# An RWKV-5 and MLP kernel on one core: k transposed by TensorE in all chunks, weights loaded one place later

## The chip, the core and the metric

The kernel runs on one core of a Trainium2 chip. The core has TensorE (PE, matrix products and transposes, results in PSUM banks), VectorE (DVE), ScalarE (ACT), GpSimd (POOL) and SyncE (SP, which here only issues DMAs), and 16 DMA engines that all its queues share. The engines run side by side, each through its own instructions in program order, and wait for one another by semaphores. The metric is the device time of the whole kernel in microseconds (us), as the median of several runs.

## The reference, cut to what matters

```python
# r, k, v: (4, 8, 768, 48); w, u: (8, 48)
for t in range(S):
    kt, vt, rt = k[:, :, t], v[:, :, t], r[:, :, t]
    cur = einsum('bhd,bhe->bhde', u[None] * kt, vt)
    y[:, :, t] = einsum('bhd,bhde->bhe', rt, state + cur)
    state = w[None, :, :, None] * state + einsum('bhd,bhe->bhde', kt, vt)
x = y.transpose(0, 2, 1, 3).reshape(4, 768, 384)
xn = (x - mean(x)) / sqrt(var(x) + 1e-06) * g_ln
out = x + maximum(xn @ w_ch1, 0.0) @ w_ch2      # 384 -> 1536 -> 384
```

A linear attention with a decaying state, then a LayerNorm and a two-layer MLP with a residual. Inputs and output are float32; the kernel multiplies in bfloat16.

## The kernel before, in words

The 4 x 768 tokens are cut into 24 chunks (also called tiles) of 128 tokens, six for each batch entry, with all 8 heads in a chunk. For chunk i:

- SyncE (in a few cases ACT) issues the loads of k and v, 192 KB each, and for every second chunk one of r (384 KB, two chunks): `load`, L182 and L188.
- k is scaled by powers of the decay into one of four buffers `sc` (`scale_k`, L359), r likewise (`scale_r`, L362). GpSimd or VectorE does it. v is cast to bfloat16 (`cast_v`, L368).
- k and r are transposed. For r, TensorE does 8 transposes for two chunks into the PSUM bank "tr" (`transposes_r`, L392), and ACT or VectorE copies them out as `rT` (L398). For k there are two ways. In chunks 0 to KP - 1 TensorE does 4 transposes into "tr" (chunk 0: bank "y"; `transposes_k`, L377) and ACT or VectorE copies them to `kT` (`evacuate_k`, L381). In chunks KP and up one DMA on SyncE's queue transposes the buffer straight into `kT` (`transpose_k_by_dma`, L385). KP is 14.
- TensorE multiplies kT and rT to scores ("at", L412). VectorE or GpSimd forms the product q (L405) for the bonus term, TensorE sums it (L433), ACT copies it out (L444), and GpSimd multiplies it with v to `Vb` (L448). VectorE masks the scores to `A` (two halves, L423). TensorE updates the state (L455, L464), VectorE decays it to `Z` (L475). TensorE forms the output y of the chunk (L487, L499), VectorE mixes it with Vb to x (L512).
- ACT centers x to `xn` (L525) and takes the squares (L532), GpSimd the reciprocal deviation `rs` (L538, L541). xn is transposed to `xT`: in tiles below LNP = 8 by TensorE through bank "tr" (L563, copied out at L575), in the others by a DMA on SyncE's queue (`ln_by_dma`, L571).

The MLP works on groups of tiles: six groups of one tile, then nine of two. Up projection in pieces of one PSUM bank "hp" (`up`, L588), ReLU on ACT (L599), down projection in three pieces per tile (`down`, L614), then VectorE combines with rs and x (L624) and SyncE or ACT issues the store (L635). One such up or down piece takes 0.65 us of TensorE.

w_ch1 and w_ch2 come in three loads of 768 KB each (`load_w1` L210, `load_w2` L214) on SyncE's queue. Their pieces are scaled or cast to bfloat16 by whichever of ACT, VectorE and GpSimd is chosen (L343 or L341 for w1, L353 for w2).

Nothing in this order is left to the hardware. The class `Planner` (L17) holds a list of tasks, each with an engine (some with alternatives), an estimated cost, what it needs, which buffers it takes and gives back, and a priority. `order` repeatedly picks the task that can start first by these estimates, fixes its engine, and so writes out one order for each engine. The tasks `TK`, `kT`, `sck` and `lc` of the change are added in the loop at L683. Bank "tr" has one buffer: transposes of r, of k and of LayerNorm rows follow one another in it, each after the copies of the one before. Where the planner sees a gap on TensorE before the first down projection, it puts filler matmuls on the identity there (`keep_warm`, L261).

The loads go in a fixed order, `seq` (L657). N1 and N2 say at which place in the list of r, k and v loads the three loads of w1 and the three of w2 are put in:

```python
N1, N2 = 8, 13
seq[N2:N2] = [("w2l", n) for n in range(NW)]
seq[N1:N1] = [("w1l", n) for n in range(NW)]
```

The list begins r0, k0, v0, k1, v1, r2, k2, v2, k3, v3, r4, k4, v4, k5, v5 (a load of r is named by the first of its two chunks). With 8, w1 stands between v2 and k3; with 13, w2 stands between v4 and k5.

Of the kernel before, what the change touches and what calls it, by code (L numbers as in the profile page):

```python
# [16 lines left out]
class Planner:  # L17
# [12 lines left out]
    def add(self, name, eng, cost, fn, needs=(), takes=(), gives=(), pri=0, load=0.0, kind=None,  # L30
            alt=None, lands=1.9):

        t = dict(name=name, eng=eng, cost=cost, fn=fn, needs=list(needs), takes=list(takes),
                 gives=list(gives), pri=pri, load=load, kind=kind, alt=alt, lands=lands, end=None,
                 first=(eng, cost))
        self.tasks.append(t)
        assert name not in self.by_name, name
        self.by_name[name] = t  # L40
# [79 lines left out]
def kernel(  # L120
# [249 lines left out]
    def k_bank(i):  # L370
        return "y" if i < 1 else "tr"

    def transposes_k(i):
        sc = k_bufs[i % NSC].rearrange("p (q e) d -> p q (e d)", e=2)
        tk_t[i] = ps.tile([P, 2 * HP, P], BF16, name=k_bank(i))
        for q in range(HP):
            nc.tensor.transpose(out=tk_t[i][:, q, :], in_=sc[:, q, :], identity=ident[:])  # L377
# [173 lines left out]
    PM = FK // NM  # L551
    NH = 8
    LNP = 8
    KP = 14
    ot_t = {}

    def ln_transposes(i):
# [97 lines left out]


    seq = [(a, i) for e in range(NT // 2) for a, i in (("r", 2 * e), ("k", 2 * e), ("v", 2 * e), ("k", 2 * e + 1), ("v", 2 * e + 1))]  # L657
    N1, N2 = 8, 13
    seq[N2:N2] = [("w2l", n) for n in range(NW)]
    seq[N1:N1] = [("w1l", n) for n in range(NW)]  # L660
    FS = FK // NW
# [21 lines left out]
    for i in range(NT):  # L683
# [8 lines left out]
        if not half:  # L692
# [7 lines left out]
            alt=[("DVE", 0.74)])  # L700
        if i < KP:
            add(f"TK{i}", "PE", 0.24, lambda i=i: transposes_k(i), [f"sck{i}"], [(k_bank(i), ("k", i), 1)], [("sck", i)], pri=p0)
# [97 lines left out]
```

## Time and profile before

| | us |
|---|---|
| median of 5 runs | 162.99 (162.59 to 164.77) |
| profiled execution, time | 162.66 |
| profiled execution, span | 160.9 |

The profile is one execution. Its page gives the busy time of each engine, a table of 40 slices, the DMA queues, the chain of work that ended last, and groups of instructions: line, engine, operation, output <- inputs, shapes, count, then busy time, mean duration in ns of one, idle time of the engine before them and what ended most of it. Some groups that the change touches, as the page has them:

```profile
L359 POOL TENSOR_TENSOR sc<-k,Fk 128x384 bf16<-128x384 f32 x21 | 22.0, 1046 | 5.0 <-PE s L464 3.2
L405 DVE TENSOR_TENSOR q<-rT,kT 128x512 bf16<-128x512 bf16 x21 | 13.8, 660 | 3.6 <-DMA kT<-sc 2.9
L398 ACT COPY rT<-tr 128x512 bf16<-128x512 bf16 x18 | 13.0, 736 | 3.5 <-PE tr L392 1.9
...
wst<-in_moe_w_ch_dram SPq DMA_DIRECT2D x6, 768.0 KB, 7.6
...
xT<-xn SPq DMA_TRANSPOSE x16, 3.4
```

The last two are DMA issues: output <- input, the queue (SPq is SyncE's), count, size and the median time from issue to landing. Matmuls overlap one another, so the mean duration of one is longer than the distance between two. Four transposes of k (L377) pass in 0.22 us, with 0.220 us as the duration of each.

### The profile page before, as it was taken

The page shows a single profiled execution, that of the slowest core. Times are in us where ns is not written, and L with a number is a line of the kernel's source. Part 1 is how long each engine was busy: PE and PEld are TensorE (multiplying, and loading weights), DVE is VectorE, ACT ScalarE, POOL GpSimd, SP SyncE. Part 2 cuts the span into 40 slices and gives each one's busy share as a digit, 9 for nine tenths or more (in the row PEclk, how much of TensorE's full clock was granted, in tenths as well). Part 3 has the DMA queues.
Part 4 walks back from the last instruction along what each step waited for, and adds up shares of the span by engine and source line. Part 5 has one row for each costly group of instructions (what it writes and reads, how often), then busy time and mean ns, then how long its engine had stood idle before and what let it go on. Part 6 is the DMA issues. An engine that isn't in the chain of part 4 may idle for free.

```text
span 160.9 us, 4644 instructions
## 1 busy us (share of the span) xinstructions
PE 147.2 (91%) x1825; PEld 115.7 (72%) x1825; DVE 104.2 (65%) x221; ACT 102.4 (64%) x231; POOL 92.6 (58%) x139
## 2 busy tenths in 40 slices
PE   5999999699699999999996999569999999999990
PEld 5888798487488787777784787457787777776660
DVE  5779886777898679887995998857851011111322
ACT  3577896979569859678766768476666755533200
POOL 7379796587979569996988786987331000000000
PEclk9999999999999999999999999999999999999999
DMA  4999899998998999999899797764203221111122
GB/s 108 229 218 389 240 213 357 304 203 183 253 267 187 221 230 213 187 228 160 192 209 168 156 200 175 160 133 107 78 2 98 77 73 49 49 49 53 49 98 98
DMA packets 80859, 26.78 MB, mean 166 GB/s; under 512 B 75072, under 2 KB 79686, under 8 KB 80838
## 3 DMA queue, kind: packets, MB, share of 16 engines
q1 hardware_dynamic: 77046, 25.11, 68.8%
q10 hardware_dynamic: 3696, 1.38, 4.2%
q8 instruction: 14, 0.23, 0.6%
q14 instruction: 7, 0.06, 0.2%
q0 software_dynamic: 96, 0.01, 0.0%
HBM read 18.88 MB, written 4.72 MB: 147 GB/s over the span
## 4 chain that ended last, share of the span: by engine, by line
PE 53%; DMA 17%; SPq 12%; POOL 7%; DVE 4%; issue 3%; ACT 1%; DVEq 0%; POOLq 0%; ACTq 0%
PE o L614 21%; PE hp L588 19%; SPq L188 7%; DMA kT<-sc 6%; DMA wst<-in_moe_w_ch_dram 6%; DMA v<-in_v_dram 3%; SPq L182 3%; POOL sc L359 3%; PE hp L614 2%; PE at L412 2%; DMA k<-in_k_dram 2%; POOL Vb L448 2%; SPq L210 1%; PE y L499 1%; PE tr L392 1%
## 5 line engine op out<-in xcount | busy, mean ns | idle before, releaser
L588 PE MATMUL hp<-xT,w_sb 128*128 128x256 bf16 (+1 forms) x540 | 58.1, 251 | 0.2
L599 ACT ACTIVATE hT<-hp 128x512 bf16<-128x512 f32 x72 | 42.8, 598 | 19.8 <-PE hp L588 19.1
L614 PE MATMUL o<-w_sb,hT 128*128 128x384 bf16 x264 | 52.4, 326 | 1.0 <-POOL w_sb L353 1.0
L588 PEld LDWEIGHTS <-w_sb 128*128 128x128 bf16 x540 | 43.6, 98 | 8.0 <-POOL w_sb L343 0.6
L614 PEld LDWEIGHTS <-hT 128*128 128x128 bf16 x288 | 26.7, 98 | 13.5 <-issue 0.8
L624 DVE SCALAR_TENSOR_TENSOR ot<-o,rs,x 128x384 f32<-128x384 f32 x22 | 13.5, 613 | 33.7 <-PE o L614 33.5
L423 DVE TENSOR_TENSOR A<-at,mask 128x512 bf16<-128x512 f32 x48 | 31.0, 681 | 1.8 <-PE at L412 1.8
L359 POOL TENSOR_TENSOR sc<-k,Fk 128x384 bf16<-128x384 f32 x21 | 22.0, 1046 | 5.0 <-PE s L464 3.2
L448 POOL TENSOR_TENSOR Vb<-v,cc 128x384 f32<-128x384 f32 x24 | 21.1, 878 | 5.7 <-ACT cc L444 5.6
L525 ACT ACTIVATE xn<-x,sum 128x384 bf16<-128x384 f32 x24 | 14.8, 616 | 4.2 <-DVE x L512 4.2
L512 DVE SCALAR_TENSOR_TENSOR x<-y,Vb 128x384 f32<-128x384 f32 x24 | 13.2, 551 | 5.4 <-POOL Vb L448 3.3
L405 DVE TENSOR_TENSOR q<-rT,kT 128x512 bf16<-128x512 bf16 x21 | 13.8, 660 | 3.6 <-DMA kT<-sc 2.9
L398 ACT COPY rT<-tr 128x512 bf16<-128x512 bf16 x18 | 13.0, 736 | 3.5 <-PE tr L392 1.9
L532 ACT ACTIVATE sq<-x,sum 128x384 bf16<-128x384 f32 x24 | 14.6, 609 | 0.5 <-DVE x L512 0.5
L362 POOL TENSOR_TENSOR sc<-r,Fr 128x384 bf16<-128x384 f32 x12 | 12.6, 1050 | 3.7 <-ACT Fr L303 2.9
L541 POOL TENSOR_TENSOR rs<-rs,expo 128x1 f32<-128x1 f32 x24 | 13.5, 564 | 2.0
L261 PE MATMUL o<-ident 128*128 128x128 bf16 x154 | 12.7, 238 | 1.6 <-DVE ident L236 1.6
L412 PE MATMUL at<-rT,kT 48*128 48x128 bf16 x192 | 9.5, 219 | 2.8 <-DMA kT<-sc 2.8
L261 PEld LDWEIGHTS <-ident 128*128 128x128 bf16 x154 | 10.5, 108 | 1.9 <-DVE ident L236 1.6
L475 DVE TENSOR_TENSOR Z<-s,WLZ 128x384 bf16<-128x384 f32 x20 | 11.0, 548 | 0.3 <-ACT cc L444 0.2
L362 DVE TENSOR_TENSOR sc<-r,Fr 128x384 bf16<-128x384 f32 x12 | 9.7, 805 | 0.4 <-ACT Fr L303 0.3
L538 POOL TENSOR_SCALAR rs<-sqs 128x1 f32<-128x1 f32 x24 | 5.3, 221 | 7.6 <-ACT sq L532 6.1
(81 smaller groups left out, 173.4 us busy)
## 6 DMA issues: line engine op xcount, KB each, us to landing
r<-in_r_dram SPq DMA_DIRECT2D x12, 384.0 KB, 4.6
k<-in_k_dram SPq DMA_DIRECT2D x24, 192.0 KB, 4.1
wst<-in_moe_w_ch_dram SPq DMA_DIRECT2D x6, 768.0 KB, 7.6
v<-in_v_dram SPq DMA_DIRECT2D x21, 192.0 KB, 4.3
out_dram<-ot SPq DMA_DIRECT2D x20, 192.0 KB, 3.4
out_dram<-ot ACTq DMA_DIRECT2D x4, 192.0 KB, 1.9
v<-in_v_dram ACTq DMA_DIRECT2D x3, 192.0 KB, 5.3
xT<-xn SPq DMA_TRANSPOSE x16, 3.4
```

Source lines behind the costliest of these rows:

```text
L261: nc.tensor.matmul(out=warm[:, :P], lhsT=ident[:], rhs=ident[:], start=True, stop=True)
L359: eng.tensor_tensor(out=k_bufs[i % NSC][:, :, :D], in0=k_t[i][:], in1=Fk[:], op=ALU.mult)
L362: eng.tensor_tensor(out=r_bufs[e % NSR][:, j, :, :D], in0=r_t[e][:, :, j * D : (j + 1) * D], in1=Fr[:, j], op=ALU.mult)
L405: eng.tensor_tensor(out=q_t[i][:], in0=rT_t[i][:], in1=kT_t[i][:], op=ALU.mult)
L423: nc.vector.tensor_tensor(out=A_t[i][:, par], in0=at_t[i][:, par], in1=mask[:].unsqueeze(1).to_broadcast([P, HP, P]), op=ALU.mult,)
L448: nc.gpsimd.tensor_tensor(out=Vb_t[i][:], in0=vf_t[i][:], in1=cc_t[i][:].unsqueeze(2).to_broadcast([P, H, D]), op=ALU.mult)
L525: nc.scalar.activation(out=xn_t[i][:], in_=x_t[i][:], func=ACT.Identity, bias=sum_t[i][:], scale=-float(C))
L532: nc.scalar.activation(out=sq[:], in_=x_t[i][:], func=ACT.Square, bias=sum_t[i][:], scale=-float(C), accum_out=sq_t[i][:])
L541: nc.gpsimd.tensor_tensor(out=rs_t[i][:], in0=rs_t[i][:], in1=expo[:], op=ALU.pow)
L588: nc.tensor.matmul(out=hp[:, f * gw : (f + 1) * gw], lhsT=w1_sb[:, n, kc, fb * P : (fb + 1) * P], rhs=xT_t[g][:, kc, :gw], start=(kc == 0) ...
L599: nc.scalar.activation(out=hT_t[g][:, nf * m : nf * (m + 1), :gw], in_=hp_t[g, m][:].rearrange("p (f t) -> p f t", f=nf), func=ACT.Relu,)
L614: nc.tensor.matmul(out=o_t[i][:, :C], lhsT=hT_t[g][:, fk, j * P : (j + 1) * P], rhs=w2_sb[:, fk, :], start=(fk == 0), stop=(fk == FK - 1),)
```

## The change

```diff
@@ -551,7 +551,7 @@
     PM = FK // NM
     NH = 8
     LNP = 8
-    KP = 14
+    KP = 24
@@ -655,7 +655,7 @@
     seq = [(a, i) for e in range(NT // 2) for a, i in (("r", 2 * e), ("k", 2 * e), ("v", 2 * e), ("k", 2 * e + 1), ("v", 2 * e + 1))]
-    N1, N2 = 8, 13
+    N1, N2 = 9, 14
     seq[N2:N2] = [("w2l", n) for n in range(NW)]
     seq[N1:N1] = [("w1l", n) for n in range(NW)]
```

With KP = 24, which is the number of chunks, the branch at L706 with `transpose_k_by_dma` is never taken: chunks 14 to 23 get a `TK` task (four transposes on TensorE) and a `kT` task (one copy by ACT or VectorE) like the chunks before them. LNP stays at 8, so the rows of LayerNorm are transposed as before, by DMA from tile 8 on. N1 = 9 puts k3 ahead of w1, and N2 = 14 puts k5 ahead of w2. The planner works with the new list of tasks from the start, so the order of all engines and some choices of engine differ from early on, also where no changed task stands.

## The prediction

> **What bounds the kernel now.** I read the busy shares, then stretches of the span, then TensorE's waits, then the chain of waits.
>
> ```profile
> PE 147.2 (91%) x1825; PEld 115.7 (72%) x1825; DVE 104.2 (65%) x221; ACT 102.4 (64%) x231; POOL 92.6 (58%) x139
> PEclk9999999999999999999999999999999999999999
> ```
>
> TensorE is the bound on average, at full clock in every slice. So what counts is TensorE's work plus the time it stands idle. The table by stretches says where that is (columns: stretch; its length; busy time of PE, weight load, DVE, ACT, POOL with instruction counts; clock; DMA share; GB/s):
>
> ```profile
> 22.00:38.00 16.00, 14.34 (x230) 11.95 (x228) 11.85 (x25) 12.79 (x30) 11.33 (x17) 1.00 1.00 261
> 38.00:46.00 8.00, 6.55 (x99) 5.12 (x98) 7.13 (x12) 5.36 (x14) 7.34 (x11) 1.00 1.06 242
> 46.00:76.00 30.00, 29.99 (x404) 23.43 (x404) 24.83 (x50) 23.73 (x56) 23.51 (x34) 1.00 1.10 212
> 76.00:90.00 14.00, 12.49 (x180) 9.72 (x180) 12.18 (x25) 9.48 (x24) 11.68 (x18) 1.00 1.03 182
> 90.00:108.00 18.00, 14.68 (x204) 11.52 (x201) 15.01 (x32) 12.29 (x32) 15.21 (x23) 1.00 0.82 163
> 108.00:157.00 49.00, 48.90 (x424) 35.97 (x424) 14.99 (x28) 24.06 (x48) 7.65 (x14) 1.00 0.22 67
> ```
>
> From 46 to 76 us and from 108 to 157 us TensorE never rests. From 76 to 108 us it lacks 1.51 + 3.32 = 4.83 us; that is where k comes through the DMA. From 22 to 46 us it lacks 1.66 + 1.45 = 3.11 us. TensorE's waits in the whole span:
>
> ```profile
> PE at L412 <- DMA kT<-sc: 2.8, 2, 1.4
> PE s L433 <- POOL q L405: 1.8, 1, 1.8
> PE s L433 <- DVE q L405: 1.1, 2, 1.0
> PE o L614 <- POOL w_sb L353: 1.0, 1, 1.0
> PE tr L563 <- DVE kT L381: 0.6, 1, 0.6
> PE tr L377 <- DVE rT L398: 0.4, 1, 0.4
> ```
>
> 2.8 us are waits of the score matmuls for a transposed k, and 0.16 us of the DVE row are a q that waited for one. The 1.8 us at 102 us are another thing: chunk 20's q stood on GpSimd (1.15 us) behind a bonus product of 1.14 us, with kT there since 101.8. Together 4.8, the whole late idleness. The other rows lie before 46 us. The chain of waits (start, length, what) shows the same from the other side:
>
> ```profile
> 80.82 6.74 DMA kT<-sc
> ...
> 104.49 3.56 DMA kT<-sc
> ```
>
> The first transpose took 6.74 us from its issue, where the median of the ten is 3.6.
>
> **The change, part by part.** The program order of the changed kernel, put beside the old one, gives the counts.
>
> *Transposes of k.* Ten DMA transposes go (L385); TensorE gets 40 more transposes (L377: 56 to 96). Four pass in 0.22 us in the chain ("PE tr L377 x4"), so 40 x 0.055 = **+2.2 us**, all on the path, as TensorE has no rest to hide it once the waits are gone. The Trainium skill ("VectorE: DVE Perf Modes", The three transpose paths) gives 390 ns for one such transpose on TensorE and 1309 ns by the DMA's crossbar; 40 x 390 ns would be an estimated 15.6 us and make the change a clear loss, but the trace's spacing is seven times shorter. The clock stood at 1.00 from 46 to 76 us, with seven chunks' transposes of k in between. The skill also says ("TensorE: Matmul & The Clock Gate", Part 4: PE-mode transpose) that transposes don't count as busy for the clock gate; by that more of them could lower the clock, which that row doesn't bear out.
>
> *The late waits.* No TensorE work waits for a DMA of k any more, and the only two q that the new order gives GpSimd belong to the first eight chunks: up to **-4.8 us**. What is late next? k now needs bank "tr" (one buffer, shared with r's transposes) and a copy on ACT (0.58 us) or VectorE (0.42 us). The nearest row is 46 to 76 us: chunks 7 to 13 took this very route and TensorE lacked 0.01 us in 30. But VectorE gets fuller. Counts by mean durations: VectorE +7 k scalings (0.74), -4 r scalings (0.81), -2 casts (0.64), +3 kT copies (0.42), +6 rT copies (0.73), +1 q (0.66), +2 weight pieces (1.0 together) = +8.0 us; GpSimd -7 and +4 scalings (1.05), -2 casts (0.66), -1 q (1.15) = -5.6; ACT +7 kT copies (0.58), -6 rT copies (0.74), +4 casts (0.51), -2 weight pieces (1.2) = +0.5. From 46 to 108 us VectorE was busy 52.0 of 62 us, 84%; with about 4.5 of the 8.0 us there, and five more feed-forward pieces (0.65 us each) ahead of the last chunk's output, it comes to 56.5 of 62 - 4.8 + 2.2 + 3.3 = 62.7, 90%. In one stretch it was already busy throughout and TensorE lost nothing (same columns):
>
> ```profile
> 90.00:95.00 5.00, 5.00 (x77) 3.92 (x75) 5.00 (x11) 3.31 (x9) 4.83 (x7) 1.00 0.83 172
> ```
>
> So new stalls between 0 and 4.8 us; I take **+0.8**, near the 46-to-76 row.
>
> *SyncE.* The ten transposes' issues go (median 1.38 us, some 14 us together) and the 10.8 us that SyncE waited in front of them, with loads of k and v queued behind. These loads come earlier; nobody but GpSimd and ACT waited for them, so I give that nothing. Three more stores and two fewer loads sit on ACT's queue, two of the stores among its ReLUs, about 0.5 us of issue each; ACT is under 80% busy there. If that cover failed, it is 1 us.
>
> *w1 and w2 one load later.* A load of k (192 KB, issued in 0.63 us, median) goes ahead of each on SyncE; at the 261 GB/s of 22 to 38 us that is 0.75 us. The first down projection started at 29.03 us after 0.96 us of waiting for a w2 cast. The new order puts the same work before it plus one k transpose (0.22 us) and ten more filler matmuls. So it starts at about 29.8 with 0.22 us more done: **+0.5 us**; fillers cost nothing, as they fill a wait for w2 (0.6 us at 57 ns each if they don't). For w1 the third piece landed at 19.5 and comes at 20.3; its up projection ran at 21.84, behind fillers that can absorb the shift: between 0 and +0.75, I take 0.
>
> *29 to 46 us.* TensorE lacked 2.15 us here (3.11 less the 0.96 at 28 us), waiting for data of chunk 6, whose k and v landed only at 37.9 and 38.2. Bytes ahead of them are unchanged, so they land no earlier. But the new order has 11 feed-forward pieces between the outputs of chunks 5 and 6 where the old one had 5. Between 0 and -2.15, maybe a loss if the fuller VectorE (it now scales k of chunk 6 and r of 6 itself, ahead of chunk 5's mix) holds up TR3; I take half, **-1.1**.
>
> *Sum.* +2.2 - 4.8 + 0.8 + 0.5 - 1.1 = -2.4 us. The last 3.9 us (final combine and stores) are unchanged. The profiled execution took 162.66 (span 160.9 and 1.76 around it), 0.33 under the median of 162.99; 162.66 - 2.4 = **160.3**.
>
> **Rivals.**
> *Slower: bank tr as the new wait.* From chunk 14 on 10 k transposes and 4 of r hand one bank over; TensorE waits for each copy. Price: the 0.57 us that a transpose waited for a kT copy at 31.3 us (in the waits as 0.6), x 14 = 8.0. With -3.2 from the other terms that is +4.8: 167.5. It decides from 5.2 us of stall, 0.37 a handover. For it: both tr rows above, and VectorE at 90%. Against: eleven handovers of that bank between 46 and 76 us (k, r and LayerNorm rows) without loss.
> *No change: the waits only move.* If data, VectorE or GpSimd are nearly as late as kT was, half of the 4.8 stays: +2.2 - 2.4 + 0.8 + 0.5 - 1.1 = 0, 162.7. For it: GpSimd waited 0.90 us for k at 100 us and ACT 3.25 us for v at 105. Against: these loads had queued behind the transposes on SyncE.
> *Little gain: the weights' delay.* No gain from 29 to 46 us and 0.75 us more for w1: -0.55, 162.1.
> That the change does nothing can be left out: the new order has no L385. The 16 transposes of LayerNorm rows by DMA are in both kernels.
>
> **How the numbers follow.** Within 1% of the median is what a measurement can't tell from no change: 161.4 to 164.6. My forecast has 0.66, from 158.4 (all idleness after 29 us gone: +2.2 - 4.8 - 2.15 + 0.5) to 161.4; the two rivals without change 0.20 together; the tr bank 0.14. For 8 in 10 the range goes from 157.8 (0.6 under the best sum, for spread and what I don't see) to 163.8, where half the late waits stay and nothing is won before 46 us (+2.2 - 2.4 + 0.8 + 0.5 = +1.1). Faster 0.66, same 0.20, slower 0.14.
>
> **What would show it.** Right: PE busy near 149.5 us (147.2 + 2.2, fillers aside), kT written by 24 copies, no PE wait for kT over 0.5 us, under 1 us idle in the chunks from 14 on, the first L614 matmul near 29.8 us. Wrong: a row of TensorE at L377 or L392 waiting for copies of kT or rT that adds up to several us (the first rival); waits of L433 for q or of L499 for A, which would say VectorE is the bound; the first L614 after 31 us.

## The result and the profile after

| | before, us | after, us |
|---|---|---|
| median of these runs | 163.47 (161.72 to 167.75, 95 runs) | 163.21 (160.91 to 167.07, 53 runs) |
| profiled execution, time | 162.66 | 162.76 |
| profiled execution, span | 160.9 | 160.7 |

The ratio is 0.9957, with a 95% interval of 0.9939 to 0.9975: the change makes the kernel 0.4% faster, about 0.7 us. The ratio compares only the faster runs, those within 1.5% of each kernel's fastest, and so isn't the quotient of the medians above. The forecast was 2.4 us. What was forecast to go did go. But the profile says that nearly as much came back, and where.

The page of the kernel after, busy shares and granted clock:

```profile
PE 150.0 (93%) x1875; PEld 117.9 (73%) x1875; DVE 107.5 (67%) x234; ACT 103.1 (64%) x234; POOL 87.5 (54%) x133
PEclk9999999999999999999999999999999999999999
```

TensorE has 2.8 us more to do than before, and the span is 0.2 us shorter; so it rests 3.0 us less. The same stretches as before (columns: stretch; length; busy time of PE, weight load, DVE, ACT, POOL; clock; DMA share; GB/s):

```profile
22.00:38.00 16.00, 15.31 (x256) 13.04 (x253) 13.38 (x29) 13.63 (x33) 12.76 (x19) 1.00 1.02 265
38.00:46.00 8.00, 8.00 (x113) 6.34 (x110) 6.92 (x13) 5.92 (x14) 4.43 (x7) 1.00 1.08 254
46.00:76.00 30.00, 29.18 (x410) 22.84 (x408) 25.42 (x55) 23.24 (x57) 26.36 (x37) 1.00 0.99 209
76.00:90.00 14.00, 11.98 (x155) 9.10 (x153) 10.98 (x22) 10.29 (x26) 10.42 (x17) 1.00 0.89 190
90.00:108.00 18.00, 16.73 (x219) 13.07 (x218) 13.82 (x31) 12.49 (x30) 10.74 (x18) 1.00 0.39 96
```

The second column less the third is TensorE's idle time. It fell from 3.11 to 0.69 us between 22 and 46 us, rose from 0.01 to 0.82 us between 46 and 76 us, and fell only from 4.83 to 3.29 us (2.02 + 1.27) between 76 and 108 us, the stage that the change was forecast to empty. TensorE's waits in the kernel after:

```profile
PE hp L588 <- ACT hT L599: 1.7, 1, 1.7
...
PE hp L588 <- ACT cc L444: 1.3, 1, 1.3
PE tr L377 <- DVE rT L398: 0.9, 2, 0.5
PE hp L588 <- POOL w_sb L343: 0.3, 1, 0.3
PE y L499 <- DVE A L423: 0.3, 1, 0.3
PE o L614 <- DVE w_sb L353: 0.3, 1, 0.3
PE o L614 <- DVE ot L624: 0.2, 1, 0.2
```

The rows of L412 waiting for kT and of L433 waiting for q are gone. In their place stand two rows of ACT, which was no releaser at all before: an up projection (L588) twice had to wait until ACT had read its PSUM bank. By the times, the row with `cc` is such a wait too: that copy ended at 95.42 us, when the up projection had begun (95.41), while the ReLU before it ended at 95.36, 0.05 us ahead, as in the first row (ReLU to 86.55, up projection from 86.60). ACT is 64% busy, so it isn't full; it waits itself. Its timeline (start, length, engine, line, operation; in brackets the idle time just before and its releaser):

```profile
84.38 0.51 ACT L368 CAST vv<-v 128x384 bf16<-128x384 f32 x1 [2.73 <-DMA v<-in_v_dram]
...
85.31 0.14 ACT L444 COPY cc<-s 128x8 f32<-128x8 f32 x1
...
85.97 0.58 ACT L599 ACTIVATE hT<-hp 128x512 bf16<-128x512 f32 x1
...
93.85 0.51 ACT L368 CAST vv<-v 128x384 bf16<-128x384 f32 x1 [2.38 <-DMA v<-in_v_dram]
...
94.78 0.58 ACT L599 ACTIVATE hT<-hp 128x512 bf16<-128x512 f32 x1
95.26 0.16 ACT L444 COPY cc<-s 128x8 f32<-128x8 f32 x1
```

and TensorE's, seen beside it:

```profile
86.60 0.82 PE L588 MATMUL hp<-xT,w_sb 128*128 128x256 bf16 x6 [1.75 <-ACT hT L599]
...
95.41 0.82 PE L588 MATMUL hp<-xT,w_sb 128*128 128x256 bf16 x6 [1.27 <-ACT cc L444]
...
107.86 0.33 PE L464 MATMUL s<-vv,sc 128*128 128x96 bf16 x4
```

L368 is `cast_v`, which turns a chunk's v to bfloat16 (the planner's task `vc`, on ACT, GpSimd or VectorE). ACT works in its written order, so it stood from 81.65 to 84.38 us at the cast of chunk 20, for a v that hadn't landed, with the copy `cc` and the ReLU `hT` of other chunks written behind it. Nobody was in a hurry for that cast: it ended at 84.89 us, and the first matmul that reads it, chunk 20's state update (the last line above), ran 23 us later. Why v came late is on SyncE's queue:

```profile
76.14 0.78 SPq L188 DMA_DIRECT2D v<-in_v_dram  x1
76.96 1.18 SPq L188 DMA_DIRECT2D k<-in_k_dram  x1
78.25 2.00 SPq L571 DMA_TRANSPOSE xT<-xn  x1
80.35 1.64 SPq L188 DMA_DIRECT2D v<-in_v_dram  x1
```

The buffer for chunk 20's v was free at 76.0 us, when GpSimd's bonus product of chunk 13 ended, but its load (the last line) stood behind a load of k and a LayerNorm transpose. The chain of waits has both late loads:

```profile
80.35 4.01 DMA v<-in_v_dram
...
90.53 3.30 DMA v<-in_v_dram
```

80.35 + 4.01 = 84.36 us, 0.02 us ahead of the cast.

### The profile page after: what moved, and what is told of

It is laid out like the page before. It is cut to its first block, busy times and chain, and to the rows that moved or that the text cites. A ratio compares the mean times of both kernels' runs of the same rounds, so it can differ in the third digit from the quotient of the medians.

```text
span 160.7 us, 4708 instructions
## 1 busy us (share of the span) xinstructions
PE 150.0 (93%) x1875; PEld 117.9 (73%) x1875; DVE 107.5 (67%) x234; ACT 103.1 (64%) x234; POOL 87.5 (54%) x133
## 4 chain that ended last, share of the span: by engine, by line
PE 39%; DMA 24%; DVE 12%; ACT 9%; SPq 6%; POOL 5%; issue 3%; ACTq 0%; POOLq 0%
PE o L614 15%; PE hp L588 15%; DMA wst<-in_moe_w_ch_dram 11%; DMA v<-in_v_dram 11%; DVE A L423 4%; SPq L188 4%; DMA k<-in_k_dram 3%; PE hp L614 2%; ACT hT L599 2%; ACT sq L532 2%; PE at L412 2%; ACT rT L398 2%; ACT xn L525 2%; DVE Z L475 1%; DVE x L512 1%
## 5 line engine op out<-in xcount | busy, mean ns | idle before, releaser
L588 PE MATMUL hp<-xT,w_sb 128*128 128x256 bf16 (+1 forms) x540 | 58.3, 251 | 3.4 <-ACT hT L599 1.7
L599 ACT ACTIVATE hT<-hp 128x512 bf16<-128x512 f32 x72 | 42.0, 596 | 14.9 <-PE hp L588 13.7
L588 PEld LDWEIGHTS <-w_sb 128*128 128x128 bf16 x540 | 43.5, 98 | 10.9 <-issue 3.5
L423 DVE TENSOR_TENSOR A<-at,mask 128x512 bf16<-128x512 f32 x48 | 30.8, 681 | 2.4 <-PE at L412 2.3
L448 POOL TENSOR_TENSOR Vb<-v,cc 128x384 f32<-128x384 f32 x24 | 21.6, 902 | 11.0 <-ACT cc L444 10.9
L362 POOL TENSOR_TENSOR sc<-r,Fr 128x384 bf16<-128x384 f32 x16 | 16.3, 1028 | 4.2 <-ACT Fr L303 2.9
L359 POOL TENSOR_TENSOR sc<-k,Fk 128x384 bf16<-128x384 f32 x14 | 14.8, 1058 | 1.0 <-DMA k<-in_k_dram 0.8
L261 PE MATMUL o<-ident 128*128 128x128 bf16 x164 | 12.8, 233 | 1.6 <-DVE ident L236 1.6
L368 ACT CAST vv<-v 128x384 bf16<-128x384 f32 x14 | 7.2, 515 | 8.0 <-DMA v<-in_v_dram 7.9
L261 PEld LDWEIGHTS <-ident 128*128 128x128 bf16 x164 | 10.6, 105 | 2.0 <-DVE ident L236 1.6
L405 DVE TENSOR_TENSOR q<-rT,kT 128x512 bf16<-128x512 bf16 x22 | 11.4, 518 | 0.9 <-ACT kT L381 0.5
L398 ACT COPY rT<-tr 128x512 bf16<-128x512 bf16 x12 | 8.7, 734 | 4.2 <-PE tr L392 2.9
L381 ACT COPY kT<-tr 128x512 bf16<-128x512 bf16 x17 | 9.9, 585 | 0.5 <-PE tr L377 0.3
```

The source lines that it names most:

```text
L261: nc.tensor.matmul(out=warm[:, :P], lhsT=ident[:], rhs=ident[:], start=True, stop=True)
L359: eng.tensor_tensor(out=k_bufs[i % NSC][:, :, :D], in0=k_t[i][:], in1=Fk[:], op=ALU.mult)
L362: eng.tensor_tensor(out=r_bufs[e % NSR][:, j, :, :D], in0=r_t[e][:, :, j * D : (j + 1) * D], in1=Fr[:, j], op=ALU.mult)
L423: nc.vector.tensor_tensor(out=A_t[i][:, par], in0=at_t[i][:, par], in1=mask[:].unsqueeze(1).to_broadcast([P, HP, P]), op=ALU.mult,)
L448: nc.gpsimd.tensor_tensor(out=Vb_t[i][:], in0=vf_t[i][:], in1=cc_t[i][:].unsqueeze(2).to_broadcast([P, H, D]), op=ALU.mult)
L588: nc.tensor.matmul(out=hp[:, f * gw : (f + 1) * gw], lhsT=w1_sb[:, n, kc, fb * P : (fb + 1) * P], rhs=xT_t[g][:, kc, :gw], start=(kc == 0) ...
```

## The experiments

Theory A: the planner wrote casts of v early into ACT's order, ahead of their loads; once TensorE no longer waits for kT, ACT standing there becomes its wait. The other theories are named in the expectations that need them. Every ratio is to the kernel before on the same chip, with its 95% interval; chips differ (before took 163.8 to 166.0 us, median), so ratios are compared, and times only within one chip.

**Late casts.** The kernel after, with four casts written later in ACT's order.

```diff
-    for t in plan.order():
+    todo = plan.order()
+    for i in (20, 21, 22, 23):
+        t = plan.by_name[f"vc{i}"]
+        todo.remove(t)
+        todo.insert(todo.index(plan.by_name[f"kT{i}"]) + 1, t)
+    for t in todo:
```

> The changed kernel with one thing moved: ACT's casts of v20 to v23 come right after the kT copy of their own chunk, instead of some 15 us earlier. No other engine's order changes. Theory A (the gain was lost to ACT standing in order behind a cast that waits for v, with a ReLU and a small copy behind it that TensorE needs): the ACT waits for v of 2.73 and 2.38 us go, TensorE's waits of 1.75 and 1.27 us behind them go, TensorE's idle time from 76 to 108 us falls from 3.3 us to under 1, and the time falls by 2 to 3 us against the changed kernel, about 160.2. Rival B (v's landing itself sets the pace of chunks 20 to 23): TensorE waits as long in front of the state update of these chunks, and the time stays within 0.7 us. Rival C (VectorE or bank tr is next in line right behind): the idle time turns up at L499 or L377, and the time falls by less than 1 us.

Measured: 0.9776 [0.9739, 0.9812]. TensorE's idle time from 76 to 108 us fell from 3.29 to 0.39 us, and both rows of waits for ACT are gone. From 46 to 76 us it rose to 1.98 us: at 47.45 us the values matmul (L499) waited 1.35 us for A, as VectorE stood at a k scaling whose k hadn't landed. It is the same fault on another engine. The late casts didn't cause it: the run with doubled transposes below, with the casts left early, shows the same 1.35 us.

**k's part alone**: the kernel before with KP = 24 and N1, N2 left at 8, 13.

> The kernel before with KP = 24 alone; the loads stay at 8 and 13. Orders are those of the kernel before up to chunk 11. Theory A: TensorE's work grows by 2.2 us, the 4.8 us of late waits go and something near the 4 us of new late waits comes in their place, if this order too puts casts of v early on ACT; time between -0.5 and +1.5 us of the kernel before. Rival D (bank tr and VectorE are no limit and ACT's early casts are a chance of the changed kernel's order): about 2.5 us faster than before.

Measured: 1.010 [1.005, 1.015], slower. TensorE's longest wait, the timeline of VectorE that explains it, and the clock afterwards:

```profile
PE y L499 <- DVE A L423: 3.7, 2, 3.4
```

```profile
86.12 0.36 DVE L368 CAST vv<-v 128x384 bf16<-128x384 f32 x1 [4.33 <-DMA v<-in_v_dram]
```

```profile
86.00:90.00 4.00, 2.61 (x32) 2.05 (x33) 3.88 (x9) 0.07 (x1) 0.76 (x1) 0.62 0.84 203
90.00:94.00 4.00, 4.00 (x32) 2.80 (x30) 1.70 (x4) 2.95 (x7) 2.77 (x5) 0.53 0.98 194
94.00:98.00 4.00, 4.00 (x47) 2.96 (x45) 2.40 (x7) 2.72 (x5) 0.00 (x0) 1.00 0.50 124
```

Here it is VectorE that stands 4.33 us at a cast of v, with the masking (L423) behind it. After TensorE's gap of 3.45 us the granted clock (the column before the DMA share) fell to about half for 6 to 7 us, and eight score matmuls took 0.61 us instead of 0.40.

**The weights' part alone**: the kernel before with N1, N2 = 9, 14 and KP = 14.

> The kernel before with N1, N2 = 9, 14 alone; k of chunks 14 to 23 goes by DMA as before. Orders are those of the changed kernel up to chunk 11. Theory A (the place of the weights gave most of what the changed kernel won: TensorE's idle time from 22 to 46 us went from 3.1 to 0.7 us): early idle time as in the changed kernel, late waits for kT of some 4 to 5 us as before, 0.6 us of fillers more; 1 to 2 us faster than the kernel before. Rival E (early idle time is given back later whatever the order, as the chunks wait for loads): no change, within 0.5 us.

Measured: 0.994 [0.989, 0.9991]. The later place of the weights alone gives what the whole change gives. Idle time from 22 to 46 us is 0.97 us. Late waits remain, 1.9 us for a q and 1.6 us for kT, but less than the 4 to 5 us for kT that were expected: idle time from 76 to 108 us is 2.32 us, and 2.82 us stand between 46 and 76 us, where the kernel before had 0.01.

**k's late transposes twice**: the kernel after, chunks 14 to 23 transposing k twice over into the same bank.

```diff
-        for q in range(HP):
-            nc.tensor.transpose(out=tk_t[i][:, q, :], in_=sc[:, q, :], identity=ident[:])
+        for _ in range(1 if i < 14 else 2):
+            for q in range(HP):
+                nc.tensor.transpose(out=tk_t[i][:, q, :], in_=sc[:, q, :], identity=ident[:])
```

> The changed kernel with the four TensorE transposes of k done twice in chunks 14 to 23 (the same values into the same bank), 40 transposes more. It measures what the change's own added work costs. If TensorE's work is on the path as I took it, the time rises by 40 x 0.055 = 2.2 us over the changed kernel. If TensorE has slack among the late waits, the extra work hides in the 3.3 us of idle time from 76 to 108 us and the time rises by less than 1 us.

Measured: 1.0028 [0.9988, 1.0068], 0.7% above the change's own 0.9957, about 1.2 us, but the two weren't run side by side. It's in between, and taken up again below.

**Late casts in the kernel before**: the loop of the first experiment, over chunks 17 to 23, behind their q.

> The kernel before (k of chunks 14 to 23 by DMA) with the casts of v17 to v23 moved right behind the q of their own chunk; only the places of these casts change, on ACT and GpSimd. It asks whether early casts also held up the kernel before. Theory A says they cost it little, since TensorE's late waits there were for kT by DMA and for one q on GpSimd: within 1 us of the kernel before. If the waits of ACT for v (1.70 and 3.25 us) and of GpSimd (1.24 us) were the hidden cause of those waits too, it is faster by 2 us or more, and then k's way of transposing is not what matters.

Measured: 1.0014 [0.9974, 1.0054]: nothing. TensorE still waited 4.6 us for kT. The test is a partial one: between 46 and 110 us ACT's longest wait for v fell from 3.3 to 1.1 us, but its waits for v still add up to 4.3 us, against 4.9 in the kernel before.

**k's part with late casts**: the second experiment's kernel, casts of chunks 12 to 23 behind their kT.

> KP = 24 alone (weights at 8 and 13) with the casts of v12 to v23 right behind the kT copy of their own chunk. KP = 24 alone was 1% slower than the kernel before; its profile had a cast of v on VectorE waiting 4.33 us and one on ACT 5.55 us, and TensorE idle for 3.45 us in front of the output of a chunk. Theory A: these waits go, and the time goes from 1% above the kernel before to 1 to 2% below (some 4 us). Rival B (the loads of v are too late for the chunks themselves) or C (bank tr, VectorE): it stays above the kernel before or within 0.5% of it.

Measured: 0.9857 [0.9806, 0.9907]. The move of k goes from 1.0% slower to 1.4% faster by the place of the casts alone, though on two chips. The clock was full throughout, and no TensorE wait is over 1.6 us. Lost clock is not the main part of the difference: the mean granted clock was 0.976 to 0.987 in five of the six runs with early casts and 0.998 to 1.000 in all six with late ones, but the sixth early run, at 1.000, took 166.19 us, near the median of 166.45.

**More tasks late**: the kernel after, casts of chunks 9 to 23 behind their kT, and the k scaling that VectorE stood at near 47 us (`sck9`) behind a masking (`A61`).

> The changed kernel with the casts of v9 to v23 right behind the kT copy of their own chunk, and the scaling of k9 on VectorE behind the masking of chunk 6 instead of ahead of it. With only v20 to v23 moved, TensorE still waited 1.35 and 0.33 us for masked scores at 47 us, which stood on VectorE behind that scaling, which waited 1.88 us for its load. Theory A: these waits shrink below 0.5 us together, and the kernel is another 1 to 1.5 us faster than with v20 to v23 alone: 2.7 to 3.2% under the kernel before. If the chunk is late for another reason, there is no further gain.

Measured: 0.9726 [0.9678, 0.9775], 160.64 us against 165.39 for before. TensorE's waits at 47 us are gone, as expected. That this makes the kernel faster still isn't shown: the four late casts alone, run again below, gave the same 0.9726.

**The loads earlier, the casts left**: the kernel after, loads of v of chunks 20 to 23 two places earlier on SyncE.

```diff
+    todo = plan.order()
+    for i in (20, 21, 22, 23):
+        t = plan.by_name[f"v{i}"]
+        sp = [s for s in todo if s["eng"] == "SP"]
+        todo.remove(t)
+        todo.insert(todo.index(sp[sp.index(t) - 2]), t)
```

> The changed kernel with the loads of v20 to v23 moved two places forward on SyncE, ahead of the transposing DMA and the load or store in front of them; the casts stay where the planner put them. If the loads were late because they stood in order behind those DMAs (v20 was issued at 80.35, 4.4 us after its buffer came free at 76), the ACT waits fall below 1 us together and the gain is that of the late casts, about 2% under the kernel before. If the buffers or the DMA engines hold v back, SyncE waits instead, the transposes and stores behind come later, and the time stays within 0.5% of the changed kernel's.

Measured: 0.9783 [0.9706, 0.986]. This works on the other end of the same wait. The two casts that ACT had stood at, on its timeline:

```profile
82.50 0.51 ACT L368 CAST vv<-v 128x384 bf16<-128x384 f32 x1
...
93.11 0.51 ACT L368 CAST vv<-v 128x384 bf16<-128x384 f32 x1 [3.27 <-DMA v<-in_v_dram]
```

Chunk 20's cast no longer waits, and TensorE's 1.75 us are gone. Chunk 22's still does: its load was issued at 87.40 us instead of 90.53 but took 5.69 us instead of 3.30, and TensorE waited 1.5 us (the profile names `cc`; as above, the ReLU ahead of it ended last). So ACT's waits didn't fall below 1 us, as they should have. The ratio fits the expected 2%, but its interval is wide, and the profiled execution shows less: its span is 0.7 us under that of the kernel after, with 2.05 us idle from 76 to 108 us and 1.54 us from 46 to 76 us. What earlier loads alone are worth stays open.

**The weights' part with late casts**: the third experiment's kernel, casts of chunks 12 to 23 behind their q.

> The kernel before with the weights loaded one place later (as in the one-part run of that) and the casts of v of chunks 12 to 23 moved behind their chunk's product q. With the two earlier parts (k by TensorE everywhere: 1.010 alone, 0.986 with late casts; before with late casts: 1.001) it fills the table of both parts with casts early and late. Theory A (the early casts only hurt where k is turned by TensorE, as only there TensorE has no earlier wait of its own to stand in): late casts change nothing here, ratio 0.994 as alone (0.985 to 1.0), with the waits for kT's transposing DMA still there. Rival D (late casts are worth 2 to 3 us wherever they are, and the two parts are not tied to them): ratio near 0.978.

Measured: 0.9938 [0.9891, 0.9986], as without late casts. In its profile the waits for kT are gone, against the expectation, and other idle time is in their place (2.25 us from 76 to 108 us, with the clock at 0.85 from 90 to 108): ACT stood idle for 4.5 us up to 86.96 us, which the profile puts down to a DMA of r, with a load of k to issue and a `cc` copy next in its order. So late casts aren't a gain by themselves.

**k's transposes twice with late casts**, and **late casts without fillers**. The second leaves out the 37 filler matmuls (L261) that the planner puts in after 20 us of its plan: `if gap > 0 and t["start"] < 20`.

> After with the four late casts, and every k transposition of chunks 14 to 23 done twice (40 matmuls more on TensorE, 2.2 us at 55 ns). In the kernel after itself the doubling cost about 1.2 us, with part of it in idle time. With late casts TensorE has 0.4 us of idle time left between 76 and 108 us, so Theory A expects nearly the full price: 1.8 to 2.4 us over the late casts alone, ratio 0.989 to 0.993. Rival C (the matmuls hide under something else, as the sum's 55 ns is a spacing with loads of weights overlapped and not a price): under 1 us, ratio below 0.984.

> After with the four late casts, and without the 37 filler matmuls that the planner puts on TensorE after 20 us of its own plan (at 57 ns they take 2.1 us). If the fillers fill waits, as the prediction had it, they cost nothing: ratio as with the late casts alone, 0.974 to 0.981, and the idle time of TensorE between 20 and 31 us grows by about 2 us, or the ratio is even higher if the granted clock falls in the gaps. If they cost what they take, the time falls by up to 2.1 us, ratio 0.965 to 0.970; the ten more that the change brought would then be 0.6 us of it.

Measured: 0.9857 [0.9803, 0.9911] and 0.9858 [0.9795, 0.9921], on a chip where before took 163.88 us. Whether the 0.8% above the first experiment comes from the edits or the chip could not be told. So the late casts were run again, alone, on yet another chip:

> After with the four late casts once more, unchanged, beside its own runs of before. The first time gave 0.9776 on a chip where before took 165.99 us; on the chip of the last three runs before took 163.88 us, and two kernels with late casts gave 0.986 there. Theory A expects the time of after to fall again by 1.0 to 1.8 per cent: ratio 0.976 to 0.988, with TensorE idle under 0.8 us between 76 and 108 us and no wait of TensorE for ACT's hT or cc over 0.3 us in the profile. If the first run was luck of its chip, the ratio is near after's own 0.9957 (above 0.99).

Measured: 0.9726 [0.9676, 0.9777]. Idle from 76 to 108 us: 0.75 us. The gain repeats, but its size still came from comparing chips. The last four kernels ran on one chip (before: 163.81 us).

> The changed kernel itself, unchanged, on the chip of the next three runs. Expected from its first measurement: ratio 0.9957 (0.990 to 1.000), if the chip doesn't matter. If the chips of the other runs explain the 0.9776 and 0.9726 of the late casts, the ratio here is lower, near 0.985.

> After with the four late casts, beside after itself. By the spans of the profiles it should be 1.5 to 1.8 us under after (0.9 to 1.1 per cent); by the ratios from different chips 3.0 to 3.8 us (1.8 to 2.3 per cent). Under 0.5 per cent would say that the early casts are not the cause.

> The late casts with the k transposes of chunks 14 to 23 done twice, on the same chip: if the 55 ns are the price, 1.6 to 2.2 us (1.0 to 1.4 per cent) over the late casts alone; if most hides in the idle time of 46 to 76 us or under the spacing of other matmuls, under 0.8 us.

> The late casts without the 37 late filler matmuls, on the same chip: within 0.4 per cent of the late casts alone if the fillers only fill waits (as the prediction had it), about 2 us lower (1.3 per cent) if they cost what they take; in its first profile a gap before the first down projection brought the granted clock of 22 to 38 us to 0.89, which would cost some of it back.

| | median, us (lowest to highest) | ratio to before |
|---|---|---|
| after | 162.67 (161.62 to 163.55) | 0.9946 [0.9907, 0.9985] |
| late casts | 160.10 (159.20 to 160.52) | 0.9785 [0.9731, 0.984] |
| late casts, transposes twice | 161.07 (160.73 to 163.53) | 0.9852 [0.9788, 0.9915] |
| late casts, no late fillers | 159.97 (159.16 to 161.33) | 0.9792 [0.973, 0.9854] |

The early casts cost the kernel after 162.67 - 160.10 = 2.57 us, between the two guesses; the two ranges don't overlap. The stretches in which they act, first after, then with late casts:

```profile
76.00:90.00 14.00, 11.81 (x143) 8.61 (x141) 10.69 (x21) 9.25 (x22) 9.45 (x15) 0.91 0.88 187
90.00:108.00 18.00, 18.00 (x218) 13.98 (x216) 15.32 (x32) 13.19 (x32) 11.60 (x17) 0.97 0.45 95
```

```profile
76.00:90.00 14.00, 13.93 (x193) 10.92 (x191) 12.71 (x28) 10.76 (x26) 12.17 (x19) 1.00 1.02 198
90.00:108.00 18.00, 18.00 (x236) 14.19 (x235) 14.89 (x32) 13.57 (x33) 10.40 (x17) 1.00 0.40 101
```

2.19 us of idle time become 0.07, and this execution of after also lost clock after its gaps: 0.91 and 0.97 over the two stretches, 0.09 x 14 + 0.03 x 18 = 1.8 us of full clock. Together that is 3.9 us, about what these two profiled executions differ by (163.54 and 159.59). The transposes' second copy costs 161.07 - 160.10 = 0.97 us for 40 matmuls; the two intervals overlap, so this is a size and not a proof, but it agrees with the 1.2 us before. In the profiles TensorE's busy time grew by 1.8 us (149.8 to 151.6) and its idle time fell by 0.5. The fillers cost nothing (-0.13 us).

## Why the prediction missed

**What held.** No TensorE work waits for a DMA of k, kT is written by 24 copies, the granted clock stayed at 1.00 with the added transposes (0.999 over the profiled execution), and the rivals' tr bank is no bound: L377 waited 0.9 us in all, not 8. The late waits went as named, -4.8. The first down projection started at 29.43 us, 0.40 us later than before and with 0.22 us more done, where +0.5 was forecast.

**What failed: the term "new stalls", taken at +0.8.** The sum needed 4.1 us there: 0.82 us between 46 and 76 us and 3.29 us between 76 and 108 us, both in its stated range of 0 to 4.8. The step chose the value "near the 46-to-76 row", since chunks 7 to 13 took the same route without loss. That row showed the route of k, and there k indeed lost nothing; it didn't show what else stood in the orders of the engines after 76 us. And the forecast looked for the next wait in VectorE's fullness, the wrong place: VectorE was busy 50.2 of the 62 us from 46 to 108 us, 81% and not the 90% worked out, and TensorE waited for ACT, which was 64% busy.

**The sentence that hid it** is in the paragraph on SyncE: the loads come earlier, "nobody but GpSimd and ACT waited for them, so I give that nothing". In the kernel before, ACT's waits for v (3.25 us at 105) were harmless: no row of TensorE's waits there names ACT, and late casts, as far as they shortened these waits, change nothing (1.0014), presumably because TensorE was waiting for kT anyway. With kT out of the way they decide: k's part alone is 1.0% slower with early casts and 1.4% faster with late ones. The rival "the waits only move" had the right outcome (162.7 against 162.76 in the profiled execution) and the right hint, ACT's wait for v. It was weighed down by the argument that the loads "had queued behind the transposes on SyncE": ten of those were gone, but the 16 of LayerNorm rows still stood there, and one of them was in front of the load in question.

**The smaller terms.** From 29 to 46 us the whole 2.15 us went, not half: of the 0.69 us idle between 22 and 46 us, 0.40 lies ahead of the transpose at 28.11 us and 0.27 ahead of the first down projection. The term was -2.1, not -1.1. Its premise, that chunk 6's k and v "land no earlier", didn't hold: k6 was issued at 29.57 us instead of 32.35, and k6 and v6 were being read by 36.21 and 36.77 us, not 37.88 and 38.22. Whether that or the 11 feed-forward pieces filled the gap isn't separated. Without this 1.0 us the sum below would come out as a small loss, so that the change gains at all is in part luck. The weights' place alone (0.994) is worth what the whole change is. The fillers cost nothing, as said. The +2.2 for the transposes is more than the doubled transposes cost (0.97 and 1.2 us); 55 ns is the distance in a run of four, and about half of that showed in the time. By spans, with the weights at +0.2 (0.40 less the 0.22 us of work): 2.2 - 4.8 + 4.1 + 0.2 - 2.1 = -0.4, against -0.2 measured.

**Not settled.** No single execution gives the 2.57 us of the early casts: after's first profile has 3.29 us idle at full clock, its second 2.19 us idle at less. Lost clock is small in the runs behind these 2.57 us: the mean granted clock was 0.989 in the profiled one of the twelve runs of after, and 0.995 to 1.000 in the others. But in the kernel before it was below 0.99 in nine of 17 runs on that chip, so some of the 0.5% between before and after may be clock. And with the weights' part alone it was 0.974 to 0.989 in all 24 runs, early casts or late. What the clock took from each ratio wasn't separated. Nor is it shown why late casts took the waits for kT away in the kernel with the weights' part alone.

## What to carry over

When a wait of the bounding engine is taken away, list the other engines' own waits for loads in that stage, harmless ones too, and ask for each what is written behind it in that engine's order and who needs that. An engine that is 64% busy can still be the bound for two microseconds, if it stands at work that nobody needs yet. A planner that orders by estimates should place a task not when its input may be there, but when its output is wanted, if the order can't be changed at run time.

## What was not expected of the hardware

The granted clock can fall after gaps of under 2 us in TensorE's work. In the second execution of the kernel after, TensorE had gaps of 0.28, 0.33 and 1.53 us between 84 and 87.3 us, and then:

```profile
86.00:88.00 2.00, 0.67 (x5) 0.52 (x5) 1.76 (x5) 2.00 (x7) 1.56 (x4) 0.89 1.00 226
88.00:90.00 2.00, 2.00 (x22) 1.23 (x21) 2.00 (x3) 1.25 (x3) 1.07 (x2) 0.50 1.28 238
90.00:92.00 2.00, 2.00 (x16) 1.43 (x15) 2.00 (x5) 1.25 (x4) 1.52 (x2) 0.75 0.75 143
92.00:94.00 2.00, 2.00 (x38) 1.60 (x36) 1.69 (x4) 1.25 (x3) 1.56 (x4) 1.00 0.99 248
```

These gaps, 2.14 us in 3.3 us, were followed by some 3 us at half clock. A gap of 1.93 us in the weights' part alone was followed by a clock of 0.67 from 78 to 82 us, one of 3.45 us in k's part alone by about half clock for 6 to 7 us, while in the first execution of the kernel after a gap of 1.75 us at the same place left the clock at 1.00. The Trainium skill ("TensorE: Matmul & The Clock Gate", Part 1) says that the clock halves after one idle window of about 3.4 us, and that the window runs freely. The half clock and the chance in it agree with these runs. That a gap must be as long as the window doesn't: 1.93 us were enough once, and 1.53 us with 0.61 us of shorter gaps ahead.
